# Two-part first loads, one batch's q/k moved to the crossbar and quarter-size w_out units in a fused attention and MLP kernel

## The chip, the cores and the metric

The kernel runs on one core of one Trainium2 chip. The metric is the device time of one execution in microseconds (us). In one session on one chip the runs of the kernel before spread by 0.3 to 1.4% from lowest to highest (350.39 to 354.77 us, for one); over several chips I saw it between 350.4 and 355.7 us, so every ratio below comes from runs of the two kernels side by side. A ratio is the mean time of one kernel's fast runs over the mean of the other's fast runs of the same rounds, so it is not quite the ratio of the medians that I quote.

## The reference

Eight batches of causal attention (8 heads, 576 tokens, 64 columns a head, 16 extra "beacon" keys and values that every token sees), whose output is the input of a two-layer MLP over all 4608 tokens:

```python
scores = scale * q @ k_all.T          # k_all, v_all: 16 beacons, then 576 tokens; causal mask
x = (softmax(scores) @ v_all)         # heads side by side: x is (4608, 512)
h = np.maximum(x @ w_in, 0.0)         # w_in (512, 2048)
out = (h * h) @ w_out                 # w_out (2048, 512), result float32
```

## The kernel before

The kernel's own list scheduler (class `Order`) runs a small model of the engines before anything is emitted: every piece of work has a priority, dependencies and an assumed duration, and the order in which the model starts them becomes the fixed order of instructions on each engine. So the order is static, made from assumed times. In the traces below each engine runs through its list in that order, and so does the queue of transfers that the sync engine issues ("SP" in the profile).

The MLP works in nine chunks of 512 tokens (27.7 us of TensorE each, half `w_in`, half `w_out`); the attention of batch b is fed in between, paced by a gate on the MLP work done so far. Two routes bring q and k into transposed form:

- Batches 0 to 2: a load on the software queue (issued by Pool) that casts to bf16, then 12 small TensorE transposes for each pair of heads, then copies out of PSUM.
- Batches 3 to 7: float32 loads on the sync queue into eight staging buffers, casts by Pool, then one crossbar transpose (a transfer that transposes on its way, DMA_TRANSPOSE in the profile) for q and one for k, also issued by the sync queue.

Likewise the attention output x is transposed by TensorE for batches 0 and 1, and by five crossbar transposes on the sync queue for batches 2 to 7.

```python
    NPE = 3          # batches whose q/k are transposed by TensorE
    NXPE = 2         # batches whose x is transposed by TensorE
...
    def add_strided(b, prio):                       # route of batches 0..2
...
        step = 1 if b == 0 else 2                   # pairs of heads in one load
        for pr in range(0, HP, step):
            h = slice(2 * pr, 2 * (pr + step))
            for n, (x, t, dst) in enumerate((("k", k, ks), ("q", q, qs))):
                def emit(e, t=t, dst=dst, h=h):
                    return [nc.gpsimd.dma_start(out=dst[b % 2][:, h],
                                                in_=t[b, h].rearrange("h (p s) d -> p h s d", s=NS))]
...
    def add_trans(b, x, prio):                      # route of batches 3..7: crossbar
...
        deps = [cast[b, x, c] for c in range(NT)]
        deps += [o for p in range(HP * (b - 2), HP * (b - 1)) for o in qk_ops[p]]
        trans[b, x] = [add(f"tr{b}{x}", "SP", 3.8, emit, prio=prio, deps=deps, dma=3.2)]
...
        def gate(o):                                # when attention pair p may start
            if p < HP:
                return True
            return o.progress >= mlp_chunk_us * (LEAD + PACE * (p - HP))
...
            for half in range(2):                   # w_out: two units of 8 matmuls for 128 tokens
                def emit_s2(e, ts=ts, half=half, first=first):
                    o = ps[first["s2"].held[2]]
                    for fc in range(8 * half, 8 * half + 8):
                        nc.tensor.matmul(o, G[:, fc, ts * 128:(ts + 1) * 128],
                                         w_out_sb[:, fc, :], start=(fc == 0), stop=(fc == NFT - 1))
...
            elif b == 2 and n == 0:
                sync = [w_ops["out", 3]]            # batch 2's first sync-queue load waits for w_out
```

The softmax here doesn't subtract the row's maximum and nothing guards it: scores larger than these inputs give would overflow.

## Time and profile before

| | before |
|---|---|
| median of 3 runs | 351.49 us |
| span of the profiled execution | 349.6 us |
| TensorE (PE) busy | 335.9 us, 96% |
| TensorE share of the chain that ended last | 86% |
| PE idle before the first transpose, 5 to 46 us, tail | 4.2, about 5.5, 3.7 us |

The engine lines of the profile's page say who is full:

```profile
PE 335.9 (96%) x2980; PEld 179.5 (51%) x2980; DVE 167.9 (48%) x391; ACT 197.3 (56%) x298; POOL 82.8 (24%) x132
...
PE 86%; DMA 9%; POOL 1%; SPq 1%; issue 1%; ACT 0%; POOLq 0%; ACTq 0%
```

PE is matmuls and PEld weight loads; DVE is VectorE, ACT is ScalarE. The windows view shows the start. Its columns are the stretch in us, its length, the busy time of each engine with its number of instructions, the granted TensorE clock, the DMA share (time of all packets over the time of the 16 transfer engines, above 1 where packets overlap) and GB/s:

```profile
5.00:10.00 5.00, 3.20 (x56) 2.12 (x53) 2.65 (x6) 1.33 (x2) 3.05 (x8) 1.00 1.13 159
10.00:15.00 5.00, 3.86 (x62) 2.56 (x63) 2.32 (x6) 2.02 (x4) 1.22 (x2) 1.00 1.16 225
15.00:20.00 5.00, 3.98 (x38) 2.02 (x36) 3.60 (x14) 4.25 (x6) 2.59 (x5) 1.00 0.27 56
20.00:25.00 5.00, 4.70 (x56) 3.14 (x56) 3.96 (x18) 4.56 (x6) 4.29 (x7) 1.00 1.14 187
45.00:50.00 5.00, 5.00 (x62) 3.71 (x62) 4.07 (x13) 3.34 (x8) 2.58 (x4) 1.00 1.23 205
```

TensorE has gaps until 25 us, and transfers nearly stop at 15 to 20 us (DMA share 0.27), because the first `w_in` quarter waits for a v tile. From 46 us to the tail TensorE has no idle time, and so the change looks at two things: the holes at the start, and TensorE work anywhere.

Some lines of the timeline (start, duration, engine, line, operation, tiles, shape, count, and the idle time before it with what ended it) give marks to compare with:

```profile
4.66 1.43 PE L412 MATMUL ps<-ident,qk_area 96*64 96x96 bf16 x24 [0.28 <-DMA qk_area<-in_k_dram]
8.49 0.49 PE L515 MATMUL strip<-qT,kT 64*128 64x240 bf16 x4
26.47 0.58 PE L692 MATMUL ps<-xT,w_in 128*128 128x240 bf16 x4
35.48 0.70 PE L412 MATMUL ps<-ident,qk_area 96*64 96x96 bf16 x24
```

The same 24 transposes take 1.43 us at the start and 0.70 us later: TensorE runs at half rate at first.

```profile
93.89 0.58 PE L515 MATMUL strip<-qT,kT 64*128 64x496 bf16 x4
```

### The profile page before, as it was taken

What the parts mean: (1) busy time and instruction counts of PE and PEld (TensorE: products, weight loads), DVE (VectorE), ACT (ScalarE), POOL (GpSimd) and SP (SyncE); (2) the same over time, 40 slices, a digit from 0 to 9 for tenths busy, and PEclk for the clock granted to TensorE, in tenths of its full rate; (3) what the DMA queues carried; (4) which work ended last, traced back from release to release, by engine and by line L of the source; (5) the groups of instructions that cost most, each with busy time, mean ns of one, the idle gap of its engine ahead of it and who ended that gap; (6) DMA issues with size and microseconds to landing.
All of it is one profiled execution on the core that took longest, in us unless ns stands there. A gap on an engine that the chain in (4) does not pass through costs nothing.

```text
span 349.6 us, 7413 instructions
## 1 busy us (share of the span) xinstructions
PE 335.9 (96%) x2980; PEld 179.5 (51%) x2980; DVE 167.9 (48%) x391; ACT 197.3 (56%) x298; POOL 82.8 (24%) x132
## 2 busy tenths in 40 slices
PE   3789999999999999999999999999999999999995
PEld 2458676645454455444445875454544444444442
DVE  6477886645762576237632864266413302301300
ACT  1686775657834876467646764577436515614611
POOL 7274640472353046105250440000000000000000
PEclk9999999999999999999999999999999999999999
DMA  7989999999998999969996999240015011011002
GB/s 101 185 139 204 220 206 210 217 234 191 230 202 143 215 253 204 187 141 233 218 229 97 220 259 155 86 113 16 2 60 129 0 60 60 2 60 61 2 13 107
DMA packets 137010, 49.50 MB, mean 142 GB/s; under 512 B 123344, under 2 KB 132048, under 8 KB 136976
## 3 DMA queue, kind: packets, MB, share of 16 engines
q1 hardware_dynamic: 127472, 40.09, 55.9%
q0 software_dynamic: 9504, 8.95, 15.7%
q8 instruction: 23, 0.38, 0.5%
q14 instruction: 11, 0.09, 0.1%
HBM read 37.22 MB, written 9.44 MB: 133 GB/s over the span
## 4 chain that ended last, share of the span: by engine, by line
PE 86%; DMA 9%; POOL 1%; SPq 1%; issue 1%; ACT 0%; POOLq 0%; ACTq 0%
PE ps L727 36%; PE ps L692 34%; PE ps L563 8%; PE strip L515 7%; DMA stg<-in_v_dram 5%; DMA qk_area<-in_k_dram 4%; SPq L331 1%; DMA qk_area<-in_q_dram 1%; POOL w_in L653 1%; PE ps L412 1%; POOL vb L286 0%; PE ps L628 0%; ACT osb L284 0%; POOL qk_area L392 0%; PE ps L409 0%
## 5 line engine op out<-in xcount | busy, mean ns | idle before, releaser
L692 PE MATMUL ps<-xT,w_in 128*128 128x512 bf16 (+3 forms) x704 | 134.4, 340 | 0.0
L727 PE MATMUL ps<-w_out,g 128*128 128x512 bf16 x576 | 130.5, 379 | 0.0
L530 ACT ACTIVATE pt<-strip 128x832 bf16<-128x832 f32 (+4 forms) x128 | 104.3, 863 | 37.3 <-PE strip L515 36.9
L708 ACT ACTIVATE g<-ps 128x512 bf16<-128x512 f32 (+2 forms) x126 | 70.3, 558 | 40.9 <-PE ps L692 39.8
L692 PEld LDWEIGHTS <-w_in 128*128 128x128 bf16 x704 | 65.1, 98 | 53.9 <-issue 2.5
L727 PEld LDWEIGHTS <-g 128*128 128x128 bf16 x576 | 54.2, 98 | 63.3 <-issue 1.2
L717 DVE TENSOR_TENSOR g<-g 128x1024 bf16<-128x1024 bf16 (+2 forms) x80 | 52.7, 661 | 59.3 <-ACT g L708 57.6
L284 ACT COPY osb<-ps 128x512 f32<-128x512 f32 x33 | 19.3, 585 | 57.8 <-PE ps L727 57.8
L563 PEld LDWEIGHTS <-pt 128*128 128x128 bf16 (+1 forms) x960 | 37.3, 99 | 17.0 <-issue 8.1
L286 POOL CAST qk_area<-stg 128x512 bf16<-128x512 f32 (+2 forms) x50 | 34.1, 695 | 42.9 <-DMA stg<-in_k_dram 21.6
L563 PE MATMUL ps<-vb,pt 128*128 128x65 bf16 (+1 forms) x960 | 42.6, 197 | 0.7 <-POOL vb L286 0.4
L286 POOL CAST vb<-stg 128x512 bf16<-128x512 f32 (+1 forms) x38 | 24.0, 646 | 66.0 <-DMA stg<-in_v_dram 22.7
L540 DVE TENSOR_TENSOR pt<-pt,tri 128x1024 bf16<-128x1024 bf16 (+1 forms) x36 | 23.9, 669 | 30.2 <-ACT pt L530 30.1
L515 PE MATMUL strip<-qT,kT 64*128 64x80 bf16 (+7 forms) x400 | 37.2, 293 | 0.1
L580 DVE TENSOR_TENSOR xn<-ps,rcp 128x320 bf16<-128x320 f32 (+2 forms) x72 | 32.7, 454 | 2.6
L579 DVE RECIPROCAL rcp<-ps 128x5 f32<-128x5 f32 (+2 forms) x72 | 13.4, 186 | 39.7 <-PE ps L563 39.3
L710 DVE TENSOR_SCALAR g<-ps 128x512 bf16<-128x512 f32 (+2 forms) x34 | 21.0, 620 | 16.9 <-PE ps L692 16.0
L515 PEld LDWEIGHTS <-kT 64*128 64x128 bf16 x400 | 12.9, 97 | 16.7 <-issue 12.7
L412 PE MATMUL ps<-ident,qk_area 96*64 96x96 bf16 x288 | 12.3, 234 | 4.0 <-DMA qk_area<-in_k_dram 2.3
L286 DVE COPY kT<-ps 128x16 bf16<-128x16 bf16 (+1 forms) x24 | 9.8, 454 | 6.8 <-PE ps L412 6.7
L412 PEld LDWEIGHTS <-qk_area 96*64 96x64 bf16 x288 | 8.9, 126 | 6.3 <-DMA qk_area<-in_k_dram 2.7
L544 DVE TENSOR_TENSOR pt<-pt,tri 80x160 bf16<-80x160 bf16 x32 | 10.4, 324 | 0.0
(33 smaller groups left out, 58.1 us busy)
## 6 DMA issues: line engine op xcount, KB each, us to landing
out_dram<-osb SPq DMA_DIRECT2D x17, 512.0 KB, 3.1
stg<-in_v_dram SPq DMA_DIRECT2D x21, 256.0 KB, 5.3
stg<-in_q_dram SPq DMA_DIRECT2D x20, 256.0 KB, 5.0
stg<-in_k_dram SPq DMA_DIRECT2D x15, 256.0 KB, 5.1
w_in<-in_moe_w_in_dram POOLq DMA_DIRECT2D x4, 512.0 KB, 8.3
w_out<-in_moe_w_out_dram POOLq DMA_DIRECT2D x4, 512.0 KB, 11.0
stg<-in_v_dram SPq DMA_DIRECT2D x7, 224.0 KB, 4.8
qk_area<-in_k_dram POOLq DMA_DIRECT2D x4, 288.0 KB, 12.3
```

The costliest lines, as they stand in the source:

```text
L286: eng[e].tensor_copy(dst, src)
L412: nc.tensor.transpose(pp[64 * hj:64 * hj + 64, at + u * NP:at + (u + 1) * NP], t[b % 2][:, 2 * pr + hj, u, :], ident[0:NP, 0:NP])
L515: nc.tensor.matmul(st[:, hj, at:at + t1 - t0], kT[b % 2][hp, pr, 128 * c:128 * c + 128], qT[b % 2][hp, pr, t0:t1], start=True, stop=True,)
L530: nc.scalar.activation(pt[take_pt.held[2]][:, :, off:off + width], st[:, :, 0:width], AF.Exp, bias=0.0, scale=scale)
L540: nc.vector.tensor_tensor(out=d, in0=d, in1=tri[:, m0:m0 + m, :][:, None].to_broadcast([128, 2, m, 128]), op=ALU.min)
L563: nc.tensor.matmul(a[:, (t - tl[0]) * (D + 1):(t - tl[0] + 1) * (D + 1)], P[0:rr, hj, o:o + 128], vb[b % 2][0:rr, c, h, :], start=(c == 0) ...
L580: nc.vector.tensor_tensor(out=xn[b % 2].rearrange("p t (h d) -> p t h d", d=D)[:, tl[0]:tl[0] + nt, h], in0=a[:, :, 0:D], in1=r[:, :, None ...
L692: nc.tensor.matmul(h[:, lo - spans[0][0]:hi - spans[0][0]], w_in_sb[:, mc, ft * 128:(ft + 1) * 128], xT[:, mc, lo % RING:lo % RING + hi - lo],
L708: nc.scalar.activation(dst, h, AF.Relu, bias=0.0, scale=1.0)
L710: nc.vector.tensor_scalar(out=dst, in0=h, scalar1=0.0, scalar2=None, op0=ALU.max)
L717: nc.vector.tensor_tensor(out=d, in0=d, in1=d, op=ALU.mult)
L727: nc.tensor.matmul(o, G[:, fc, ts * 128:(ts + 1) * 128], w_out_sb[:, fc, :], start=(fc == 0), stop=(fc == NFT - 1))
```

## The change

The intent: fill the start, and take TensorE work away.

1. Batch 0's q/k come in two parts (240 and 336 tokens, four heads a load). The transposes of a batch's beacon keys are gathered into one group. The order on the software queue is part 0, the first `w_in` quarter, part 1, v tiles 2 to 4, the other `w_in` quarters, with no wait for a v tile.
2. Batch 2's q/k go by the sync queue and the crossbar, its x by TensorE (`NPE = 2`, `NXPE = 3`).
3. Small parts: `w_out` units of 4 matmuls instead of 8, and exps ahead of the relus on ACT.

```diff
+    whole_parts = [(0, NP, NS)]
+    parts_of = {0: [(0, 120, 2), (240, 112, 3)], 1: whole_parts, 2: whole_parts}
...
-    NPE = 3
-    NXPE = 2
+    NPE = 2
+    NXPE = 3
...
-        soft = b in SOFT_V
+        soft = b in SOFT_V or (b == 0 and c >= 2)
...
+    def add_part_loads(b, part, prio, after, free):
+        t0, np_, ns = parts_of[b][part]
+        step = HP // 2
...
+                    return [nc.gpsimd.dma_start(
+                        out=strided_buf(b, x, part)[:, h],
+                        in_=t[b, h, t0:t0 + np_ * ns, :].rearrange("h (p s) d -> p h s d", s=ns))]
...
-                                prio=base + i + s, deps=[qk], give=(qk, s)))
+                                prio=(base + i + s) * 1.0e-4 - 30.0, deps=[qk], give=(qk, s)))
...
-            w_ops["in", i] = add(f"win{i}", "POOL", 1.3, emit, prio=-100 + i, sync=[v_loads[0][3]] if i == 0 else (),
-                                 behind=[w_ops["in", i - 1]] if i else (), dma=3.15)
+            w_ops["in", i] = add(f"win{i}", "POOL", 1.3, emit, prio=-100 + i, behind=[v_loads[0][4]] if i == 1 else first_loads[0] if i == 0 else [w_ops["in", i - 1]], dma=3.15)
+            if i == 0:
+                first_loads.append(add_part_loads(0, 1, -95.0, [w_ops["in", 0]], []))
...
-            for half in range(2):
+            for qd in range(4):
...
-                    for fc in range(8 * half, 8 * half + 8):
+                    for fc in range(4 * qd, 4 * qd + 4):
```

More of the change, by code (lines that the diff above doesn't have):

```diff
@@ L226, with strided_buf @@
           for i in range(2)]
-    qs = [qk_area[0:NP, (2 * i) * WS:(2 * i + 1) * WS].rearrange("p (h s d) -> p h s d", h=H, s=NS)
-          for i in range(2)]
-    ks = [qk_area[0:NP, (2 * i + 1) * WS:(2 * i + 2) * WS].rearrange("p (h s d) -> p h s d", h=H, s=NS)
-          for i in range(2)]
+    whole_parts = [(0, NP, NS)]
+    parts_of = {0: [(0, 120, 2), (240, 112, 3)], 1: whole_parts, 2: whole_parts}
+    def strided_buf(i, x, part):
+        at = (2 * (i % 2) + "qk".index(x)) * WS
+        for _, _, ns in parts_of[i][:part]:
+            at += H * ns * D
+        _, np_, ns = parts_of[i][part]
+        return qk_area[0:np_, at:at + H * ns * D].rearrange("p (h s d) -> p h s d", h=H, s=ns)
     bkf = [sb("bkf", [Nb, H, D], FP32)] * 2
@@ L376, in add_beacon, with emit_tp @@
                  deps=[cast[b - 1, "bk"]] if b else [])
-        cast[b, "bk"] = add(f"bkc{b}", "DVE", 0.4, lambda e: nc.vector.tensor_copy(bks[b % 2], bkf[b % 2]), prio=prio,
-                               deps=[ld])
-        return cast[b, "bk"]
+        bk = add(f"bkc{b}", "DVE", 0.4, lambda e: nc.vector.tensor_copy(bks[b % 2], bkf[b % 2]), prio=prio,
+                 deps=[ld])
+        cast[b, "bk"] = bk
+        box = {}
+        def emit_tp(e):
+            pp = ps[box["t"].held[2]].bitcast(BF16)
+            for pr in range(HP):
+                nc.tensor.transpose(pp[:, pr * Nb:(pr + 1) * Nb], bks[b % 2][:, 2 * pr:2 * pr + 2, :], ident[0:Nb, 0:Nb])
@@ new lines, in add_beacon, with emit_ev @@
+        busy = [o for pr in range(HP) for o in qk_ops[HP * (b - 2) + pr]] if b >= 2 else []
+        box["t"] = add(f"tpb{b}", "PE", 0.45, emit_tp, prio=prio - 100.0, deps=[bk, ident_op], take=("ps", "tp"))
+        def emit_ev(e):
+            pp = ps[box["t"].held[2]].bitcast(BF16)
+            copy_on(e, kT[b % 2][:, :, 0:Nb], pp[:, 0:HP * Nb].rearrange("p (g n) -> p g n", g=HP))
+        bk_ev[b] = add(f"ekb{b}", "DVE", 0.2, emit_ev, prio=-200.0, deps=[box["t"]] + busy, give=box["t"])
+    bk_ev = {}
@@ new lines, in add_part_loads, with emit @@
+    def add_part_loads(b, part, prio, after, free):
+        t0, np_, ns = parts_of[b][part]
+        step = HP // 2
+        for pr in range(0, HP, step):
+            h = slice(2 * pr, 2 * (pr + step))
+            for n, (x, t) in enumerate((("k", k), ("q", q))):
+                def emit(e, t=t, x=x, h=h):
+                    return [nc.gpsimd.dma_start(
+                        out=strided_buf(b, x, part)[:, h],
+                        in_=t[b, h, t0:t0 + np_ * ns, :].rearrange("h (p s) d -> p h s d", s=ns))]
+                o = add(f"sld{b}{x}{part}.{pr}", "POOL", 0.75, emit, prio=prio + pr + 0.1 * n, behind=after,
+                        deps=free, dma=1.84 * np_ * ns / S)
+                after = [o]
+                for i in range(step):
+                    strided[b, part, pr + i, x] = o
+        return after
@@ L381, in add_strided @@
     def add_strided(b, prio):
-        loads = {}
-        bk = add_beacon(b, prio)
-        after = [w_ops["in", 3]] if b == 1 else [strided[b - 1][HP - 1, "q"]] if b else []
+        add_beacon(b, prio)
         free = trans[b - 2, "q"] + trans[b - 2, "k"] if b >= 2 else []
         trans[b, "q"], trans[b, "k"] = [], []
-        step = 1 if b == 0 else 2
-        for pr in range(0, HP, step):
-            h = slice(2 * pr, 2 * (pr + step))
-            for n, (x, t, dst) in enumerate((("k", k, ks), ("q", q, qs))):
-                def emit(e, t=t, dst=dst, h=h):
-                    return [nc.gpsimd.dma_start(out=dst[b % 2][:, h],
-                                                in_=t[b, h].rearrange("h (p s) d -> p h s d", s=NS))]
-                o = add(f"sld{b}{x}{pr}", "POOL", 0.65 * step, emit, prio=prio + pr + 0.1 * n, behind=after,
-                        deps=free, dma=0.92 * step)
-                for i in range(step):
-                    loads[pr + i, x] = o
@@ L398, in add_strided @@
-        strided[b] = loads
-        for pr in range(HP):
-            h = slice(2 * pr, 2 * pr + 2)
-            box = {}
-            busy = qk_ops[HP * (b - 2) + pr] if b >= 2 else []
-            def emit_tp(e, x, pr=pr, h=h, box=box):
-                pp = ps[box[x].held[2]].bitcast(BF16)
-                t, at = (ks, Nb) if x == "k" else (qs, 0)
-                if x == "k":
-                    nc.tensor.transpose(pp[:, 0:Nb], bks[b % 2][:, h, :], ident[0:Nb, 0:Nb])
-                for u in range(NS):
-                    for hj in range(2):
-                        nc.tensor.transpose(pp[64 * hj:64 * hj + 64, at + u * NP:at + (u + 1) * NP],
-                                            t[b % 2][:, 2 * pr + hj, u, :], ident[0:NP, 0:NP])
-            for n, x in enumerate("kq"):
-                box[x] = add(f"tp{b}.{pr}{x}", "PE", 0.65 if b else 0.9, lambda e, x=x, f=emit_tp: f(e, x),
-                             prio=100.0 * (HP * b + pr) - 190 + 0.1 * n,
-                             deps=[bk if x == "k" else None, loads[pr, x], ident_op] + busy, take=("ps", "tp"))
-            def emit_k(e, pr=pr, box=box):
-                pp = ps[box["k"].held[2]].bitcast(BF16)
-                copy_on(e, kT[b % 2][:, pr, 0:Nb], pp[:, 0:Nb])
-                copy_on(e, kT[b % 2][:, pr, Nb:Nb + S].rearrange("p (n s) -> p n s", s=NS),
-                        pp[:, Nb:Nb + S].rearrange("p (s n) -> p n s", s=NS))
-            def emit_q(e, pr=pr, box=box):
-                pp = ps[box["q"].held[2]].bitcast(BF16)
-                copy_on(e, qT[b % 2][:, pr, 0:S].rearrange("p (n s) -> p n s", s=NS),
-                        pp[:, 0:S].rearrange("p (s n) -> p n s", s=NS))
-            ek = add(f"ek{b}.{pr}", "DVE", 0.85, emit_k, prio=-200.0, deps=[box["k"]], give=box["k"])
-            eq = add(f"eq{b}.{pr}", ("DVE", "ACT"), 0.7, emit_q, prio=-199.0, deps=[box["q"]], give=box["q"])
-            trans[b, "k"].append(ek)
-            trans[b, "q"].append(eq)
@@ new lines, in add_strided, with emit_tp, emit_ev @@
+        if b > 0:
+            after = [w_ops["in", 3]] if b == 1 else [strided[b - 1, 0, HP - 1, "q"]]
+            add_part_loads(b, 0, prio, after, free)
+        for part, (t0, np_, ns) in enumerate(parts_of[b]):
+            n_tok = np_ * ns
+            for pr in range(HP):
+                h = slice(2 * pr, 2 * pr + 2)
+                busy = qk_ops[HP * (b - 2) + pr] if b >= 2 else []
+                groups = ["kq"] if 2 * n_tok <= 1024 else ["k", "q"]
+                for n, xs in enumerate(groups):
+                    box = {}
+                    def emit_tp(e, xs=xs, pr=pr, box=box, part=part, np_=np_, ns=ns, n_tok=n_tok):
+                        pp = ps[box["t"].held[2]].bitcast(BF16)
+                        for i, x in enumerate(xs):
+                            for u in range(ns):
+                                for hj in range(2):
+                                    at = i * n_tok + u * np_
+                                    nc.tensor.transpose(pp[64 * hj:64 * hj + 64, at:at + np_],
+                                                        strided_buf(b, x, part)[:, 2 * pr + hj, u, :], ident[0:np_, 0:np_])
+                    tp = add(f"tp{b}.{part}.{pr}{xs}", "PE", 0.75 if b == 0 else 0.6, emit_tp,
+                             prio=100.0 * (HP * b + pr) - 190 + 0.1 * n + 1000.0 * part,
+                             deps=[strided[b, part, pr, x] for x in xs] + [ident_op] + busy, take=("ps", "tp"))
+                    box["t"] = tp
+                    evs = []
+                    for i, x in enumerate(xs):
+                        def emit_ev(e, i=i, x=x, pr=pr, box=box, t0=t0, n_tok=n_tok, ns=ns):
+                            pp = ps[box["t"].held[2]].bitcast(BF16)
+                            dst, at = (kT, Nb) if x == "k" else (qT, 0)
+                            copy_on(e, dst[b % 2][:, pr, at + t0:at + t0 + n_tok].rearrange("p (n s) -> p n s", s=ns),
+                                    pp[:, i * n_tok:(i + 1) * n_tok].rearrange("p (s n) -> p n s", s=ns))
+                        ev = add(f"e{x}{b}.{part}.{pr}", ("DVE",) if x == "k" else ("DVE", "ACT"),
+                                 {"DVE": 0.12 + n_tok / 960.0, "ACT": 0.2 + n_tok / 1200.0}, emit_ev,
+                                 prio=(-200.0 if x == "k" else -199.0) + 0.01 * part, deps=[tp])
+                        evs.append(ev)
+                        trans[b, x].append(ev)
+                        trans_part[b, part, pr, x] = ev
+                    add(f"tpg{b}.{part}.{pr}{xs}", "-", 0.0, None, deps=evs, give=tp)
@@ L437 @@
+    trans_part = {}
     class Phase:
@@ L489, in gate, with deps_of @@
             return o.progress >= mlp_chunk_us * (LEAD + PACE * (p - HP))
-        if b < NPE:
-            qk_deps = [trans[b, "k"][pr], trans[b, "q"][pr]]
-        else:
-            qk_deps = trans[b, "k"] + trans[b, "q"]
-        take_pt = add(f"pt{p}", "-", 0.0, None, prio=100.0 * p, deps=qk_deps, take=("pt", "pt"), gate=gate)
+        def deps_of(part):
+            if b >= NPE:
+                return trans[b, "k"] + trans[b, "q"]
+            return [bk_ev[b]] + [trans_part[b, n, pr, x] for n in range(part + 1) for x in "kq"]
+        take_pt = add(f"pt{p}", "-", 0.0, None, prio=100.0 * p, deps=deps_of(0), take=("pt", "pt"), gate=gate)
         av_ops[p] = []
         for n, ph in enumerate(phases(b)):
-            add_phase(b, pr, p, n, ph, take_pt, qk_deps, gate)
+            add_phase(b, pr, p, n, ph, take_pt, deps_of(n if b < NSPLIT else 0), gate)
     def add_phase(b, pr, p, n, ph, take_pt, qk_deps, gate):
@@ L647, with add_weights @@
     w_ops = {}
-    def add_weights():
-        for i in range(4):
+    def add_weights(quarters):
+        for i in quarters:
             def emit(e, i=i):
@@ L722, in add_chunk, with emit_s2 @@
             prev, first = None, {}
-            for half in range(2):
-                def emit_s2(e, ts=ts, half=half, first=first):
+            for qd in range(4):
+                def emit_s2(e, ts=ts, qd=qd, first=first):
                     o = ps[first["s2"].held[2]]
-                    for fc in range(8 * half, 8 * half + 8):
+                    for fc in range(4 * qd, 4 * qd + 4):
                         nc.tensor.matmul(o, G[:, fc, ts * 128:(ts + 1) * 128],
                                          w_out_sb[:, fc, :], start=(fc == 0), stop=(fc == NFT - 1))
-                prev = add(f"s2.{j}.{ts}.{half}", "PE", 1.73, emit_s2, prio=base + 100 + 2 * ts + half,
-                           deps=[x for f in range(4 * half, 4 * half + 4) for x in sq[f]]
-                           + [w_ops["out", qd] for qd in (2 * half, 2 * half + 1)] + [prev],
-                           take=None if half else ("ps", "mlp"), pe_time=1.73)
+                prev = add(f"s2.{j}.{ts}.{qd}", "PE", 0.865, emit_s2, prio=base + 100 + 4 * ts + qd,
+                           deps=sq[2 * qd] + sq[2 * qd + 1] + [w_ops["out", qd], prev],
+                           take=None if qd else ("ps", "mlp"), pe_time=0.865)
                 first.setdefault("s2", prev)
@@ L768 @@
         lp = 10.0 * b
+        if b == 0:
+            first_loads = [add_part_loads(0, 0, -200.0, [], [])]
+            add_weights([0])
         if b < NPE:
@@ L776 @@
             if x == "v" and b == 0:
-                if c == 0:
-                    sync = [strided[0][0, "q"]]
+                if c == 2:
+                    behind = first_loads[1]
             elif x == "v" and b == 1 and c == 0:
-                behind = [strided[1][HP - 1, "q"]]
+                behind = [strided[1, 0, HP - 1, "q"]]
             elif b == 2 and n == 0:
@@ L789 @@
         if b == 0:
-            add_weights()
+            add_weights([1, 2, 3])
         if b == 1:
```

## The prediction

> **What bounds the kernel now.** TensorE. On the profile's page PE is busy 335.9 of 349.6 us and has 86% of the chain that ended last; its timeline has no idle after 46 us until the tail. Its 13.7 us of idle time: 4.2 us before the first transpose (waits: for the beacon cast), about 5.8 us in gaps from 4.7 to 45.3 us (waits: 2.3 + 1.7 us for strided k/q loads, 1.0 us for normalised x, the rest mask and v), 3.7 us at the end (last eviction and store), which nothing here touches.
>
> The start is slow for another reason too. Twenty-four transposes take 1.43 us at 4.7 us but 0.70 us at 35.5 us. This fits the Trainium skill, "TensorE: Matmul & The Clock Gate", Part 1: full rate comes only after a busy window of about 3.4 us. From such groups I estimate 5 to 6 us lost until about 22 us.
>
> Transfers nearly stop from 17.5 to 20 us (windows: DMA share 0.08), because w_in waits for a v tile; afterwards they are saturated to about 50 us.
>
> **What the change does.**
> 1. Batch 0 q/k come in a 240-token and a 336-token part, four heads a load. The first attention phase needs only 0.49 MB: all four pairs should have it by about 8 us (now 13.6), so its exps end near 12 us instead of 17. Two v tiles no longer wait for a strided load, but their casts now stand on DVE ahead of the kT copies: that can hold the first q-k near 8 us (now 8.5).
> 2. w_in quarter 0 goes ahead of part 1; v tiles 2 to 4 and the other quarters follow without a wait. The hole goes; first w_in matmuls start near 14 to 17 us (now 26.5), filling PE gaps. Against this: more and smaller packets, and part 1 arrives only near 13 to 15 us. ACT then needs about 10.6 us for its twelve exps, so batch 0 ends near 27 to 28 us, little before now (28.8); the gain is in the work done meanwhile. Estimate: 2 to 3 us from gaps and hole, 1 to 2 us from an earlier full rate.
> 3. Batch 2: off PE go 96 transposes (eight groups at 0.32 to 0.38 us) and 4 beacon ones, about 3.2 us; added are 20 x transposes, 1.4 us. Batch 0 has 80 instead of 96. Net 2 us, all critical, as PE is full there. But batch 2 now loads by the sync queue after w_out lands (now 53.8 us, then about 49): ten loads, Pool casts, two crossbar transposes of 5 to 7 us. Ready near 75 us; the order on PE wants them near 78 to 80. That is thin.
> 4. Shorter w_out units: same matmuls; about 0.
>
> **Sum.** 351.5 - 2.5 - 1.5 - 2 = 345.5, rounded to 345.8 for new stalls. Range 342.8 to 348.8. Faster by over 2% (below 344.5): 0.29; within 2%: 0.69; slower: 0.02.
>
> **What would show it.** PE busy about 332 to 334 us; idle between 5 and 46 us down from 5.8 to 2 to 4 us; no DMA hole near 18 us; first w_in matmul before 18 us; transposes at the fast rate from about 12 to 15 us; no wait of PE for kT/qT of batch 2 near 75 us; last 3.7 us unchanged.
>
> **What would make it wrong.** Part 1 landing after 16 us because small cast packets are slow (then 348 or more); batch 2's crossbar late (a stall of several us near 75 us); DVE's in-order v casts delaying the first phase; or full rate from 9 us on (then 343).

## More of the kernel before

Last, the sync queue's own timeline, for batch 3, whose q/k are the first by the crossbar:

```profile
53.79 0.31 SPq L330 DMA_DIRECT2D stg<-in_beacon_v_dram  x1
...
61.79 0.87 SPq L330 DMA_DIRECT2D stg<-in_beacon_k_dram  x1
...
78.05 4.16 SPq L363 DMA_TRANSPOSE qT<-qk_area  x1
82.31 3.82 SPq L363 DMA_TRANSPOSE kT<-qk_area  x1
```

Batch 2 occupies this queue for 8.0 us (53.79 to 61.79, v alone). Batch 3's k crossbar is issued at 82.31 us, and its first q-k matmul stands at 93.89 us, without idle time before it: there is room.

## The result

The changed kernel took 350.71 us (median of 4 runs, 350.28 to 351.35), the kernel before 351.77 us beside it: ratio 0.9968, 95% interval 0.9944 to 0.9993. The change is worth 0.3%, a fifth of what I predicted, and the time lies outside my range.

```profile
PE 330.0 (95%) x2846; PEld 175.8 (50%) x2884; DVE 171.1 (49%) x394; ACT 191.7 (55%) x290; POOL 92.2 (26%) x139
...
PE 80%; DMA 12%; SPq 2%; issue 1%; DVE 1%; POOL 1%; ACT 1%; POOLq 0%; ACTq 0%
```

TensorE's busy time fell as expected (38 of the 2884 matmul records are missing, so 330.0 is a little low). But the chain that ended last now has 12% DMA instead of 9%, and 2% of the sync queue. The start did fill, from 10 us on, and the hole in the transfers at 15 to 20 us is gone (DMA share 0.27 before, 1.21 now); a new one is at 45 to 50 us:

```profile
5.00:10.00 5.00, 1.71 (x20) 1.00 (x20) 1.75 (x6) 0.66 (x3) 4.99 (x11) 1.00 1.32 162
10.00:15.00 5.00, 4.22 (x52) 2.62 (x54) 4.03 (x17) 3.75 (x7) 4.72 (x6) 1.00 1.44 190
15.00:20.00 5.00, 5.00 (x66) 3.02 (x66) 3.95 (x14) 3.34 (x7) 3.45 (x6) 1.00 1.21 228
20.00:25.00 5.00, 5.00 (x60) 3.42 (x57) 3.07 (x11) 3.50 (x7) 1.95 (x3) 1.00 1.24 207
45.00:50.00 5.00, 5.00 (x73) 3.81 (x72) 4.68 (x14) 3.40 (x6) 0.00 (x0) 1.00 0.70 115
```

The timeline of TensorE has the marks of the start, and two waits that the kernel before does not have:

```profile
9.43 0.49 PE L547 MATMUL strip<-qT,kT 64*128 64x240 bf16 x4 [0.49 <-ACT qT L290]
21.58 1.78 PE L725 MATMUL ps<-xT,w_in 128*128 128x240 bf16 x8
23.95 0.53 PE L547 MATMUL strip<-qT,kT 64*128 64x336 bf16 x4
25.30 0.35 PE L547 MATMUL strip<-qT,kT 64*128 64x336 bf16 x4
...
101.66 0.58 PE L547 MATMUL strip<-qT,kT 64*128 64x496 bf16 x4 [0.84 <-DMA kT<-qk_area]
128.45 0.58 PE L547 MATMUL strip<-qT,kT 64*128 64x496 bf16 x4 [1.85 <-DMA kT<-qk_area]
```

101.66 us is the first q-k of batch 3, 128.45 us that of batch 4: both wait for their k crossbar. TensorE idles 0.84 and 1.85 us there, 2.7 us together. In the view of waits of the weight loads (total us, times, longest), whose records are complete, the stretch 100 to 130 us shows 3.7 us for the two, since a weight load can pause while the matmul before it still runs:

```profile
PEld L547 <- DMA kT<-qk_area: 3.7, 2, 2.3
```

In the kernel before no wait for kT occurs in that stretch. The sync queue's timeline says why the crossbars are late:

```profile
49.70 0.31 SPq L336 DMA_DIRECT2D stg<-in_beacon_k_dram  x1
...
75.46 0.55 SPq L336 DMA_DIRECT2D stg<-in_beacon_k_dram  x1
...
96.38 3.60 SPq L369 DMA_TRANSPOSE kT<-qk_area  x1
...
122.54 4.33 SPq L369 DMA_TRANSPOSE kT<-qk_area  x1
```

Batch 2 now takes the queue from 49.70 to 75.46 us, 25.8 us instead of 8.0. Batch 3's k crossbar is issued at 96.38 us instead of 82.31, while TensorE, which has less to do, wants it earlier.

**How far ahead is TensorE?** One more measure is needed, because end times hide where a lead was won and lost. All weight loads are in the trace, one for each matmul, in the program's order. I gave each matmul the time that its shape takes at full rate and summed those that had not begun at a time t: the work left. The time of a shape is columns / 2.4 GHz + 2.5 ns, as the Trainium skill states for back-to-back matmuls ("TensorE: Matmul & The Clock Gate", "Wait — 56ns, not 53.3ns?"). This trace agrees: 216 ns is the median from one start to the next of two matmuls of 512 columns. Q-k matmuls count 0.655 of that, q/k transposes 0.69, fitted to this trace's groups. The kernel before has 317.8 us of such work, the changed one 315.9 us. The lead of a kernel at t is the work left in the kernel before at t, minus its own:

| t (us) | before: work left | after: work left | lead of after |
|---|---|---|---|
| 0 | 317.8 | 315.9 | 1.9 |
| 45 | 293.5 | 289.4 | 4.1 |
| 90 | 250.8 | 245.2 | 5.6 |
| 100 | 240.8 | 235.7 | 5.1 |
| 130 | 211.7 | 209.8 | 1.9 |
| 330 | 15.3 | 14.0 | 1.3 |

At 90 us the changed kernel is 5.6 us ahead, which is what I predicted for the end. By 130 us it has given 3.7 us of it back; TensorE's two idle times for kT are 2.7 us of that. The rest asks whether these waits are the cause, and what makes the crossbars late.

### The profile page after: what moved, and what is told of

Read it like the earlier page. It is cut to its first block, busy times and chain, and to the rows that moved or that the text cites. A ratio compares the mean times of both kernels' runs of the same rounds, so it can differ in the third digit from the quotient of the medians.

```text
span 348.6 us, 7192 instructions
## 1 busy us (share of the span) xinstructions
PE 330.0 (95%) x2846; PEld 175.8 (50%) x2884; DVE 171.1 (49%) x394; ACT 191.7 (55%) x290; POOL 92.2 (26%) x139
## 3 DMA queue, kind: packets, MB, share of 16 engines
q0 software_dynamic: 10432, 8.46, 15.3%
HBM read 37.22 MB, written 9.44 MB: 134 GB/s over the span
## 4 chain that ended last, share of the span: by engine, by line
PE 80%; DMA 12%; SPq 2%; issue 1%; DVE 1%; POOL 1%; ACT 1%; POOLq 0%; ACTq 0%
PE ps L725 32%; PE ps L760 30%; PE ps L595 8%; PE strip L547 7%; DMA kT<-qk_area 5%; SPq L643 2%; PE ps L443 2%; DMA qk_area<-in_q_dram 2%; DMA stg<-in_q_dram 2%; DMA stg<-in_k_dram 1%; DMA stg<-in_v_dram 1%; DMA xT<-xn 1%; PE ps L660 1%; DVE xn L612 0%; POOL qk_area L292 0%
## 5 line engine op out<-in xcount | busy, mean ns | idle before, releaser
L741 ACT ACTIVATE g<-ps 128x512 bf16<-128x512 f32 (+2 forms) x122 | 69.3, 568 | 42.3 <-PE ps L725 40.3
L750 DVE TENSOR_TENSOR g<-g 128x1024 bf16<-128x1024 bf16 (+2 forms) x80 | 51.5, 646 | 73.8 <-ACT g L741 72.4
L760 PEld LDWEIGHTS <-g 128*128 128x128 bf16 x576 | 52.9, 98 | 60.4 <-issue 2.4
L292 POOL CAST qk_area<-stg 128x512 bf16<-128x512 f32 (+2 forms) x60 | 41.8, 705 | 46.3 <-DMA stg<-in_k_dram 31.0
L290 ACT COPY osb<-ps 128x512 f32<-128x512 f32 x24 | 14.1, 586 | 59.1 <-PE ps L760 59.1
L743 DVE TENSOR_SCALAR g<-ps 128x512 bf16<-128x512 f32 (+2 forms) x38 | 22.1, 585 | 13.9 <-PE ps L725 12.8
L292 DVE COPY osb<-ps 128x512 f32<-128x512 f32 x12 | 8.3, 692 | 17.5 <-PE ps L760 15.5
L443 PE MATMUL ps<-ident,qk_area 96*64 96x96 bf16 (+2 forms) x176 | 8.5, 251 | 3.4 <-DMA qk_area<-in_k_dram 1.6
L290 ACT COPY qT<-ps 128x240 bf16<-128x240 bf16 (+2 forms) x9 | 3.7, 426 | 9.5 <-DVE kT L292 8.4
```

Source lines behind the costliest of these rows:

```text
L290: nc.scalar.copy(dst, src)
L292: eng[e].tensor_copy(dst, src)
L741: nc.scalar.activation(dst, h, AF.Relu, bias=0.0, scale=1.0)
L743: nc.vector.tensor_scalar(out=dst, in0=h, scalar1=0.0, scalar2=None, op0=ALU.max)
L750: nc.vector.tensor_tensor(out=d, in0=d, in1=d, op=ALU.mult)
L760: nc.tensor.matmul(o, G[:, fc, ts * 128:(ts + 1) * 128], w_out_sb[:, fc, :], start=(fc == 0), stop=(fc == NFT - 1))
```

## The experiments

Theory T: the lead is given back at crossbars of the sync queue, which batch 2 has made late. Rival R: one of the small parts (exps, `w_out` units) or the new interleaving costs it. Rival W: transfers after 50 us are a wall, and any lead is lost somewhere. (T2, in later expectations, is T with batch 3's x crossbars as a second such place.) The table gives each kernel's lead in the profiled execution, beside the measured ratio to the kernel before. The lead is that of one execution, and executions of one kernel differ by 1 us and more, so only larger differences are read.

| kernel | ratio (95% interval) | lead at 45 | 90 | 130 | 140 | 160 | 330 us |
|---|---|---|---|---|---|---|---|
| after | 0.9968 (0.9944 to 0.9993) | 4.1 | 5.6 | 1.9 | 1.9 | 1.8 | 1.3 |
| y10_start_only | 0.9966 (0.9941 to 0.9992) | 1.3 | 1.9 | 1.7 | 1.5 | 1.6 | 1.7 |
| x2_only_b2 | 1.0242 (1.0206 to 1.0279) | 2.2 | 2.7 | 1.2 | 0.7 | -8.3 | -9.5 |
| x16_small | 1.0067 (1.0025 to 1.0109) | 0.4 | 0.2 | 0.2 | -0.5 | -1.6 | -2.4 |
| x1_b2soft (start, small) | 1.0029 (1.0000 to 1.0059) | 1.5 | 1.7 | 1.3 | 1.5 | -2.2 | -2.2 |
| x12_start_b2 | 1.0151 (1.0110 to 1.0191) | 3.9 | 5.2 | 3.8 | 3.7 | -4.2 | -5.0 |
| x3_late | 1.0314 (1.0287 to 1.0341) | 4.5 | 5.9 | 4.7 | 4.9 | -9.1 | -11.5 |
| x4_w1 | 0.9952 (0.9925 to 0.9979) | 4.6 | 5.6 | 2.1 | 1.9 | 1.9 | 1.9 |
| y7_warm | 0.9991 (0.9968 to 1.0013) | 4.9 | 6.0 | 2.1 | 2.1 | 1.9 | 1.1 |
| x13_lat5 | 1.0005 (0.9957 to 1.0053) | 5.0 | 6.2 | 3.0 | 2.8 | 0.5 | 0.6 |
| y9_x4 | 1.0050 (1.0021 to 1.0079) | 3.1 | 4.6 | -1.1 | -2.9 | -2.6 | -2.6 |
| y6_gates_x4 | 0.9943 (0.9910 to 0.9975) | 2.7 | 4.0 | 3.5 | 1.9 | 1.8 | -1.1 |
| x11_thin_v (wrong result) | 0.9859 (0.9816 to 0.9903) | 4.2 | 5.6 | 4.9 | 4.6 | 4.8 | 4.9 |
| z6b_w1_places | 1.0040 (1.0002 to 1.0078) | 4.6 | 5.8 | 4.3 | 3.9 | -3.1 | -3.3 |
| z1_w1_gates | 1.0047 (1.0017 to 1.0078) | 2.8 | 4.1 | 3.4 | 3.4 | -3.3 | -3.5 |
| z7_x5 | 0.9904 (0.9860 to 0.9948) | 2.1 | 3.2 | 2.7 | 2.9 | 2.8 | 2.8 |
| z7_x8 | 0.9999 (0.9960 to 1.0037) | -0.1 | 0.8 | 0.2 | -0.1 | -0.2 | 0.2 |

### The parts alone and in pairs

**x1_b2soft**: the change without its batch 2 part.

```diff
-    NPE = 2
-    NXPE = 3
+    NPE = 3
+    NXPE = 2
```

> The whole change with one part undone: batch 2's q/k again by the software queue and TensorE transposes, its x by crossbar. Theory T (the lead won at the start was given back at waits of TensorE for the k crossbar of batches 3, 4 and 7, because batch 2 now occupies the sync queue): no wait for kT at 101 and 128 us; about 1.8 us more TensorE work, about 4.3 us of lead not given back; time near 348.2. Rival R (the give-back comes from the other parts: exps before relus, w_out units cut to quarters, the changed interleaving): time near 350.7 + 1.8 = 352.5, slower than the kernel before.

Measured: 352.57 us. The waits for kT are gone, as T says, but the time is what R says. The lead of 1.5 us holds until 140 us and is lost at one place: 2.08 us of idle time at 151.10 us, before the fourth MLP chunk's first matmul, for the x crossbar of batch 3. (The lead falls by more than the wait, from 1.5 to -2.2 us, because the granted clock then drops to 0.50 from 153 to 155 us; more on this under z6b.) So there is a second place where a lead can be lost, and T in its first form is too narrow.

**x2_only_b2**: the kernel before, with only batch 2's route changed (the same two numbers, 2 and 3).

> The kernel before with only batch 2's route changed (q/k by crossbar, x by TensorE). Theory T: 1.8 us less TensorE work, but waits for kT of batch 3 and 4 as in the changed kernel or longer, since w_out lands later: near 353, slower than or equal to before. Rival R: no harm, only the saved work: near 350.0.

Measured: 360.12 us, far slower than either theory said. Of T's two claims, the harm is there, but its place is another: batch 3's x again, 7.75 us at 157.47 us.

**y10_start_only**: the change's start alone (x1_b2soft with exps and `w_out` units as before).

> x1_b2soft with exps and w_out units also as in the kernel before: only the start of the change is left. If these two parts do nothing: equal to x1_b2soft, about 352.6 (1.003 of before), with a lead of about 1.5 us at 100 us and a wait for xT of batch 3 near 150 us. If the shorter w_out units or the exp priority caused the xT wait: below 350.

Measured: 351.36 us, ratio 0.9966. TensorE waits for no crossbar after 60 us, and the lead of 1.3 to 1.9 us stays to the end. So the start alone gives all that the whole change gives. Against x1_b2soft (1.0029), with the same start, the small parts cost 0.6%: the xT wait of x1_b2soft is not there without them.

**x16_small**: the kernel before with the small parts alone.

> The kernel before with exps ahead of relus and quarter w_out units only. TensorE's work is the same: 351.7 if nothing else moves. x1_b2soft against y10_start_only says that these parts cost up to 2 us when they place batch 3's x crossbar behind more loads: then a wait for xT near 150 us and 352 to 354.

Measured: 354.21 us. The waits for xT appear, 1.01 us at 152.02 us and 0.56 us at 190.55 us, but they are smaller than the loss; the rest of it is spread, and I did not trace it. R is half right: the small parts do cost something by themselves.

**x12_start_b2**: start and batch 2, without the small parts.

> The changed start and batch 2's new route, but exps and w_out units as before. If the b2 route by itself wipes out the lead as in x2_only_b2: waits for xT or kT, 353 or more. If exps and w_out units have no part in it: as the whole change, 350.7.

Measured: 357.04 us (one of its six runs was slow; the five fast ones have a median of 356.69 us). TensorE waits for batch 3's x:

```profile
152.92 1.87 PE L725 MATMUL ps<-xT,w_in 128*128 128x512 bf16 x4 [6.20 <-DMA xT<-xn]
```

The static order explains most of this. In the changed kernel's sync queue the five x crossbars of batch 3 stand ahead of batch 5's q crossbar and are issued from 142.66 us; here they stand behind it, from 147.73 us. The small parts, harmful alone, happen to shift the order so that the batch 2 route hurts less. The parts don't add up: alone they are worth -0.3%, +2.4% and +0.7%, together -0.3%.

### Does a larger or smaller lead matter?

**y7_warm**: the whole change plus 14 matmuls on zeros while TensorE has nothing to do.

```diff
+    nc.vector.memset(g[1][:, NFT - 1, :], 0.0)
+    for _ in range(14):
+        nc.tensor.matmul(ps[3], g[1][:, NFT - 1, 0:128], g[1][:, NFT - 1, :], start=True, stop=True)
```

> The whole change plus 14 idle-time matmuls (128x512, on zeros, result unused) before the first transpose, which raise TensorE to its full rate early. The start should gain 2 to 4 us by 25 us. T2 and W both say that the lead is then given back at longer kT waits: 349.5 to 350.5. If the kT waits were only incidental: near 347.5.

Measured: 352.11 us. The start gained less than I thought, 0.9 us by 25 us (work left 306.8 against 307.7). The added lead, 0.8 us at 45 us, was down to 0.2 us at 130 us, and the waits for kT grew from 3.1 to 3.8 us. So most of a lead won earlier is waited away.

**x4_w1**: batch 2's loads start earlier.

```diff
-                sync = [w_ops["out", 3]]
+                sync = [w_ops["out", 1]]
```

> The whole change, but batch 2's loads wait for the second w_out quarter to land, not the fourth. Theory T: loads start some 4 us earlier than 49.7 us and fill the hole at 45 to 53 us (DMA share 0.7 there now); kT of batch 3 and 4 lands earlier, but the static order also moves their q-k about 2.6 us of MLP work earlier, so only part of the waits goes: 348 to 350. If w_out becomes late instead, TensorE waits for w_out near 52 us and the time is 350.7 or more.

Measured: 349.95 us. The kT waits went from 3.1 only to 2.9 us, since the scheduler's model saw earlier data and moved the q-k matmuls forward too.

### What makes the crossbar late?

**x11_thin_v**: a wrong result. The order of instructions is that of the changed kernel on every engine, but v tiles of batches 2 to 4 load 16 rows.

```diff
+            if x == "v" and b in (2, 3, 4):
+                some = 16
+                insts.append(queue.dma_start(out=st[lo:lo + some],
+                                             in_=t[b, :, t0:t0 + some, :].transpose([1, 0, 2])))
+                return insts
```

> Wrong result on purpose: the whole change, with the same order of instructions on every engine, but each v tile of batches 2, 3 and 4 loads 16 rows in place of up to 128, so about 3 MB less is moved between 60 and 120 us. If the bytes moved make the k crossbar of batches 3 and 4 late (W): these land earlier, the waits for kT near 101 and 128 us go, the lead of 5.6 us at 90 us stays to the end: near 346.5. If the length of the sync queue's list of issues, casts by Pool or the order on TensorE holds it: waits stay, 350 or more.

Measured: 346.92 us, ratio 0.9859. The page shows 34.18 MB read instead of 37.22. No wait for kT is left at all, and the lead of 5.6 us at 90 us is still 4.9 us at 330 us. This is all that TensorE waits for from 60 to 345 us:

```profile
PE ps L765 <- issue: 0.5, 3, 0.2
```

The sync queue has the same entries in the same order, but they come through sooner:

```profile
60.23 1.84 SPq L339 DMA_DIRECT2D stg<-in_v_dram  x4
...
89.63 3.10 SPq L374 DMA_TRANSPOSE kT<-qk_area  x1
...
112.81 3.88 SPq L374 DMA_TRANSPOSE kT<-qk_area  x1
```

The k crossbars of batches 3 and 4 are issued at 89.63 and 112.81 us instead of 96.38 and 122.54. This is the cleanest of the tests: TensorE's list is unchanged, nothing but part of the v transfers was taken away, and the lost time came back. So the v transfers between 50 and 130 us (their bytes, or their packets, which were cut together) make the crossbars late, and late crossbars take the lead.

How they do it is only half shown. In the changed kernel the sync queue never pauses: from batch 2's first load (49.70 us) to batch 3's k crossbar (96.38 us) it runs entries for 43.9 of 46.7 us, and the longest gap between two entries is 0.06 us. In x11_thin_v the same entries run for 37.6 of 40.4 us; those of the nine v loads fell from 8.7 to 3.7 us. So the crossbar is late by the time of the entries ahead of it. What sets that time is open: the work of issuing, or transfer engines that are too full to take more (their share is 1.09 from 55 to 130 us in the changed kernel and still about 1.07 in x11_thin_v). The test cut both, and so does not refute the rival in its own expectation, the length of the sync queue's list. The Trainium skill, "DMA: Bandwidth & Descriptors", "Issuing engines are not separate DMA queues", calls the sequencer's time to start a transfer usually small beside the transfer. Here it is not: after 50 us the entry of a 128-row load of q, k or v takes 0.4 to 3.0 us, and that of a q or k crossbar 3.1 to 4.4 us, of a median of 6.5 (q) and 5.5 us (k) from issue to landing.

### Can the order alone be mended?

**x3_late**: q-k of batches 3 to 7 half a chunk later, so that TensorE has MLP work where it waits.

```diff
-            return o.progress >= mlp_chunk_us * (LEAD + PACE * (p - HP))
+            return o.progress >= mlp_chunk_us * (LEAD + PACE * (p - HP) + (0.5 if p >= 3 * HP else 0.0))
```

> The whole change, but q-k matmuls of batches 3 to 7 may start only half a chunk (about 14 us of MLP work) later in the static order; transfers and work are the same. Theory T: the waits for kT go, as MLP matmuls fill that time: near 346.7. Rival R: 350.7 as the changed kernel. A second rival, that the transfers themselves set the pace (any order waits somewhere else, for xT or g): 350 or more with a new wait.

Measured: 362.67 us. The waits for kT shrank from 3.1 to 0.6 us and the lead at 140 us was 4.9 us, as T says. Then one wait lost everything:

```profile
159.23 5.87 PE L725 MATMUL ps<-xT,w_in 128*128 128x512 bf16 x16 [13.64 <-DMA xT<-xn]
```

Later attention makes batch 3's x later. In this order its x crossbars stand behind batch 5's loads and both its q/k crossbars, and are issued at 154.11 us.

**x13_lat5**: the scheduler assumes a longer time from a transfer to its use (5.0 us for 1.6), which puts the same matmuls later by its own rules.

> The whole change, but the list scheduler that fixes the order assumes 5.0 us instead of 1.6 us from a transfer to its use, so it places q-k of batches 3 and 4 later (after 54.6 and 69.2 us of MLP work instead of 51.1 and 67.5). T2: the kT waits shrink from 3.1 to under 1 us and the time is 347 to 349. W: the wait moves to xT of batch 3 or kT of a later batch: 350 to 352.

Measured: 351.64 us. Batch 3 no longer waits for kT, but batch 4 (1.82 us) and batch 5 (1.76 us) do. That is what W expects.

**y9_x4** and **y6_gates_x4**: batch 3's x by TensorE (`NXPE = 4`), without and with a milder, tapering delay of q-k.

```diff
+ (max(0.0, 0.55 - 0.075 * (p - 3 * HP)) if p >= 3 * HP else 0.0)     # inside the gate, y6 only
```

> The whole change with only batch 3's x moved to TensorE. T2: kT waits near 101 and 128 us stay, 1.0 us of work added: 351 to 352. If the x crossbar alone was what held the lead back: 348 or less.

> The whole change with two edits: q-k matmuls of batches 3 and 4 gated later by up to half a chunk of MLP work, tapering to none by batch 5 (a milder form of x3_late), and batch 3's x transposed by TensorE too, so that the start of the fourth MLP chunk does not wait for a crossbar. Theory T2 (the lead of 5.6 us at 90 us is given back because the static order puts q-k of batches 3 and 4 at the moment the crossbar is just late, and because x of batch 3 stands behind loads in the sync queue): both waits go, 1.0 us of TensorE work is added: near 347.4. Rival W (transfers after 50 us are a wall that any lead meets somewhere): a new wait appears and the time stays at 350 or more.

Measured: y9_x4 353.53 us; the wait for batch 4's kT grew to 4.44 us. y6_gates_x4 349.96 us: better than the changed kernel, but not by what T2 expected. Its profiled execution, the slowest of its six, waits 1.37 us for batch 4's kT and 2.80 us, at 189.31 us, for batch 4's x.

**z6b_w1_places** and **z1_w1_gates**: earlier loads of batch 2 (as x4_w1), and gates that hold q-k of batches 3 and 4 at their places in the changed kernel, or a little later.

```diff
-                sync = [w_ops["out", 3]]
+                sync = [w_ops["out", 1]]
...
+ {12: 0.40, 13: 0.28, 14: 0.15, 15: 0.03, 16: 0.12}.get(p, 0.0)      # inside the gate, z6b
+ (max(0.0, 0.444 - 0.075 * (p - 3 * HP)) if p >= 3 * HP else 0.0)    # inside the gate, z1
```

> The whole change, batch 2's loads wait for the second w_out quarter (about 3 us earlier), and gates put q-k of batches 3 and 4 back to the places that they have in the changed kernel (after 50.2 and 67.5 us of MLP work). If arrival against place is the cause: kT waits fall from 3.1 to under 1 us, and the lead of 5.6 us at 90 us mostly stays: 347 to 348.5. But batch 3's x crossbar now stands behind one q crossbar: if that binds, a wait for xT near 148 us and 349.5 to 351.

> As z6b_w1_places, but q-k of batches 3 and 4 some 2 us of MLP work later still (52.0 and 70.1). kT waits gone; batch 3's x is normalised later, so the wait for xT near 148 us is more likely: 347 if not, 350 or more if so.

Measured: 353.71 and 353.85 us. In z6b the waits for kT fell to 1.0 us and the lead was 3.9 us at 140 us; in z1 there were none. But then both lost about 7 us between 140 and 160 us, at batch 3's x. In z6b, TensorE's timeline and the windows after it:

```profile
150.83 1.87 PE L725 MATMUL ps<-xT,w_in 128*128 128x512 bf16 x4 [4.54 <-DMA xT<-xn]
...
164.46 1.03 PE L725 MATMUL ps<-xT,w_in 128*128 128x512 bf16 x4
```

```profile
150.00:155.00 5.00, 4.17 (x23) 2.00 (x23) 0.00 (x0) 0.60 (x1) 0.00 (x0) 0.50 0.59 116
155.00:160.00 5.00, 5.00 (x45) 2.36 (x43) 2.68 (x6) 2.81 (x4) 0.61 (x1) 0.83 0.88 226
```

The wait costs more than its 4.54 us: after it the granted clock is 0.50, and four matmuls take 1.87 us that take 1.03 us later. In these traces a stretch at 0.50 follows every wait of 4.4 us or more (x2, x3, x12, y9, z6b, z1), and of the shorter ones only x1's of 2.08 us; the two of the changed kernel were not followed by one.

The sync queue's timeline holds the link:

```profile
138.20 2.99 SPq L337 DMA_DIRECT2D stg<-in_v_dram  x4
141.30 4.24 SPq L369 DMA_TRANSPOSE qT<-qk_area  x1
145.63 6.43 SPq L643 DMA_TRANSPOSE xT<-xn  x5
```

Batch 5's q crossbar is next in the list. It starts right after the v loads, keeps the queue for 4.24 us, and only then may batch 3's x go, 3 us later than in the changed kernel (142.66 us), while TensorE is 2 us further ahead. (The view of the queue's waits puts 3.6 us of waiting for Pool at this q crossbar. That is no wait: Pool's last cast of batch 5's q and k ends at 141.29 us, just before the entry starts, and the casts of v that the view names end while it runs.)

**z7_x5** and **z7_x8**: z6b with x of batches 0 to 4, or of all batches, by TensorE (`NXPE = 5`, `NXPE = 8`).

> z6b with x of batches 3 and 4 transposed by TensorE too. Adds 2.0 us of TensorE work to the whole change. If crossbars in the sync queue are all that takes the lead: no wait over 1 us after 60 us, 350.7 - 4.3 + 2.0 = 348.4. If not: a wait for kT of a later batch or for xT of batch 5, 350 or more.

> z6b with x of all batches transposed by TensorE: 5.0 us more TensorE work than the whole change and no x crossbar at all. If crossbars are all that takes the lead: no late wait, near 351.4; slower than z7_x5 by 3 us, if z7_x5 has no late wait.

Measured: z7_x5 348.60 us (expected 348.4), ratio 0.9904; z7_x8 352.02 us (expected 351.4). In both, TensorE has no wait over 0.2 us after 60 us. The whole list of waits of z7_x5's TensorE from there on:

```profile
PE ps L760 <- issue: 0.6, 4, 0.2
PE ps L725 <- issue: 0.2, 1, 0.2
```

So in a kernel with a right result the lead stays (3.2 us at 90 us, 2.8 us at 330 us) once no crossbar on the way to TensorE is late. That goes against W in its strong form, that any lead is lost somewhere. (These kernels differ from the changed one in three things, x, gates and earlier loads, so they test T as a whole and no single edit.) The price is countable: three more batches of x, z7_x8 against z7_x5, cost 3.4 us, about 1.1 us each. z7_x5 has the lowest ratio of all right kernels here, 0.9904, and its median is below that of both kernels; it was timed beside the kernel before, not beside the changed one.

## Why the prediction was wrong, point by point

- **What bounds the kernel: right, but only for the kernel before.** TensorE was full from 46 us on. I took that for a property of the program; it was one of a margin. Batch 3's k crossbar was issued 11.6 us before its first use (82.31 and 93.89 us). In the changed kernel, where TensorE waited for it, the first use came 5.3 us after the issue (5.9 us for batch 4); so I estimate from these that some 6 of the 11.6 us were slack.
- **Step 1, the start: mechanism right, gain half.** I expected the first q-k near 8 us; it came at 9.43 us (8.49 before). I expected first `w_in` matmuls at 14 to 17 us; they came at 21.58 (26.47 before). Idle time from 5 to 46 us fell from about 5.5 to 4.1 us, at the edge of "2 to 4". By 45 us the changed kernel had won 4.1 - 1.9 = 2.2 us of lead besides the work saved, and the start alone 1.3 us (y10_start_only); I had counted 2.5 + 1.5.
- **The earlier full rate: wrong.** I expected it at 12 to 15 us. The same four 336-column q-k matmuls take 0.53 us at 23.95 us and 0.35 us at 25.30 us. Before, by the same kind of group, the step lies near 25 to 26 us, so my "until about 22 us" was off too. The term "1 to 2 us" was at most that small shift.
- **Step 3, batch 2: its own check held, its consequence failed.** w_out landed as expected (loads start at 49.70 us; I said about 49). Batch 2's first q-k at 77.15 us shows no idle time before it, so "thin" was enough. But I looked at batch 2 alone. The 17.8 us that it adds to the sync queue (25.8 against 8.0) pushed batch 3's k crossbar back by 14.1 us and batch 4's by 5.9 us, and there TensorE waited. I had written "Net 2 us, all critical, as PE is full there"; what it rested on, that TensorE stays full, was undone by the same step.
- **Step 4, the w_out units, "about 0": wrong in isolation.** Together with the exp priority they cost 0.7% on the kernel before (x16_small), by changing the static order. I tested them only together.
- **The sum: the step that failed.** "351.5 - 2.5 - 1.5 - 2" books each gain at the end of the program, as if a lead could not be lost on the way; that is where step 3's "all critical, as PE is full there" failed. At 90 us the lead was 5.6 us, and with the lead kept the time is 346.9 us (x11_thin_v), inside my range. Of the 5.6 us, 3.7 us were gone by 130 us and 0.6 us more by 330 us. TensorE's idle times at the two k crossbars are 2.7 us of the 3.7; x11_thin_v, which has no such wait, lost 0.7 us over the same stretch, so about 3 us are theirs. That the 5.6 us equal my sum is partly luck: 1.9 us are saved work, 2.2 us came by 45 us where I had counted 4, and 1.5 us came between 45 and 90 us, which I had not counted and did not trace.

What stays open: how much of x16_small's loss is due to which small part; whether the sync queue's entries are slow because of the work of issuing or because the transfer engines are full, and whether bytes or the number of small packets count, which x11 cut together; and a mended order that keeps the whole 5.6 us, for which I found none with a right result.

## What to carry to other kernels

A gain at the start of a static schedule is a lead, and counts only if nothing later is due at a fixed time: before booking it, list for each later input when it arrives and when it is first used, and compare the smallest margin with the lead. Moving work off the full engine on to a queue that runs in order shifts everything behind it on that queue, so the batches to check are the next ones, not the one moved; add up the time of the entries on that queue, and look whether it has gaps to take more. And parts of a change to a list scheduler's inputs don't add up: test them alone and in pairs, and compare the work left over time rather than the end times.

## What the Trainium skill lacked or had wrong

- "TensorE: Matmul & The Clock Gate", Part 1, gives about 3.4 us of sustained busy time until the full rate. In the changed kernel TensorE is busy 4.22 of 5 us from 10 to 15 us and 5.00 of 5 us from 15 to 20 us, and is still at half rate at 23.95 us. In y7_warm the 14 dense matmuls did raise it (four 240-column q-k matmuls take 0.34 us at 9.35 us, and 0.49 us again at 12.21 us), but the clock was granted at 0.50 from 12 to 20 us, although the profile calls TensorE busy for 7.60 of these 8 us:

```profile
9.00:12.00 3.00, 1.76 (x34) 1.24 (x34) 2.65 (x9) 2.41 (x5) 3.00 (x5) 0.99 1.29 196
12.00:15.00 3.00, 2.60 (x37) 1.52 (x32) 2.58 (x11) 2.28 (x4) 2.73 (x4) 0.50 1.58 194
15.00:18.00 3.00, 3.00 (x42) 1.73 (x40) 2.21 (x10) 1.97 (x4) 2.22 (x5) 0.50 1.13 245
18.00:20.00 2.00, 2.00 (x26) 1.03 (x24) 1.75 (x6) 1.42 (x3) 1.19 (x3) 0.50 1.30 188
```

  These stretches hold transposes, q-k and attention-times-v matmuls, and the first `w_in` matmuls come just after them. That such mixes don't count as busy is an inference; Part 4 of that page says so of transposes alone.
- Part 1 of that page, "Seeing it yourself", warns that the trace's clock events are unreliable, but does not give this form of it: the clock record reads 1.00 at the start while the matmuls run at half rate (before and after, 5 to 20 us: 1.00 in the windows; before, 1.43 us for 24 transposes that later take 0.70 us). The record there isn't proof of the rate; the time of a known group is.
- "DMA: Bandwidth & Descriptors", in the section cited under x11_thin_v, takes the issuing of a transfer to be usually small. The sync queue was full with issuing (43.9 of 46.7 us from 49.70 us on), and in z6b_w1_places one q crossbar's entry of 4.24 us stood before x crossbars that TensorE then waited 4.54 us for.
